# Converting one layer's weights first, by column blocks, and ten chunks of the other layer's a batch later

## The chip, the cores and the metric

The kernel runs on one core of one Trainium2 chip. The metric is the device time of one execution in microseconds (us), the median of several runs. An execution has five engines with queues of their own: PE (matrix multiply; its weight loads are shown apart, as PEld), DVE (vector), ACT (activation functions and copies), POOL (general vector work) and SP, which here only issues DMA transfers. Each engine works its own queue in the order in which the program wrote it; the waits between engines are semaphores.

## The reference, cut to what matters

```python
def _attn_ref(q, k, v):                      # q, k, v: (8, 8, 576, 64) = batch, head, token, width
    scores = np.matmul(q, k.transpose(0, 1, 3, 2)) / np.sqrt(64)
    kth = np.partition(scores, -32, axis=-1)[..., -32:-31]
    scores = np.where(scores >= kth, scores, -1e9)
    attn = np.exp(scores - max); attn /= sum
    return attn @ v

def _moe_ref(x, w_ch1, w_ch2):               # x: (8, 576, 512); w_ch1: 512 x 2048; w_ch2: 2048 x 512
    u = x + np.real(np.fft.fft(np.fft.fft(x, axis=1), axis=2))
    un = (u - mean) / sqrt(var + 1e-6)
    return u + np.maximum(un @ w_ch1, 0.0) @ w_ch2
```

Attention keeps the 32 largest scores of each row; its output, with the heads side by side, goes through the Fourier mix and a two-layer network. The two weight matrices are given as 64-bit floats, while q, k and v have 32 bits.

## The kernel before, in words

**Tiles and steps.** A batch has 8 heads, taken in four pairs; a pair has nine tiles of attention rows (`IN_PAIR`, L292). So a batch has 36 tiles (`PER_BATCH`), all eight have 288 (`N`). The main loop (L1348) takes one step per tile. A step `i` emits, among other things: the score matmuls of tile `i+3` (`scores`, L300) and the copies of them to `S` on ACT; the mask (`mask`, L394: ACT at L397, then POOL at L400) and the exponentials (`expo`, L402, ACT) of an earlier tile; PE's transposes of the result (`transposes`, L411); and on DVE the search for the 32 largest (`top_ops`, L366), which is the last half for tile `i` and the first half for tile `i+1`: four MAX8 (L381) and three MATCH_REPLACE8 (L383) in a step. `bounds` (L386) then makes two small numbers per row on POOL (`nt`), which mask and exponentials need.

In the first batch (`short`, L1353) the exponentials of a step come ahead of the matmuls and the mask follows the search in the same step. From the second batch on, mask and exponentials of tile `i-1` both lie in step `i`, with ACT's part of the mask after the score copies and the exponentials at the end of the step.

**The second half of a batch** follows `T0`, some steps after its last tile: folds, a Fourier transform by matmuls (`dft_tokens`, `dft_channels`), statistics, and then the network. `hidden` (L823) multiplies by `w1` and ACT applies the Relu; `back` (L852) multiplies by `w2`. These network matmuls are units in `queue`, and each step takes as many of them as the planner (`level`, L1321) gives it, so that PE has other work beside the next batch's attention. In the first batch there are no such units yet.

**Weights.** As the matrices have 64-bit numbers, each chunk of 128 rows by 512 columns is loaded raw and converted by six operations (`weight_steps`, L165): `scale_high` and two in `rest` on ACT, `shift` on DVE, and two `join` on POOL. There are 32 chunks, 16 of `w1` and then 16 of `w2`, in the order of rows. Chunk `n` is converted in step `34 * n // 32 + 1` (`start_of`, L1187), so in all but two of the steps 1 to 34 of the first batch. The raw words lie in five slots of one space (`sp1`), and at the end of the step a load for chunk `n + 5` is issued on SP, once the slot is free.

**Centring.** `un` is not centred; instead the mean over the rows is taken off each column of `w1`. `centre(c)` (L1200) does it for 512 columns: 4 matmuls with a matrix of ones, one copy on ACT to `mean`, and 4 subtractions on POOL. Two of the four blocks are centred in the first batch (in steps 19 and 27, a subtraction in each of the four steps after), the others in steps 36 and 37, with all four subtractions of each in step 39 and 40.

**Order.** `at(step, where, fn)` puts work into a plan, and the loop runs it at fixed places of the step: "convert" at the step's head (ACT), "pe" among its matmuls, "shift" after the third operation of the first search half (DVE), "join" inside the mask of the first batch, between ACT's part and POOL's, and "pool" and "load" at the step's end. `parts_of_w2` (L779) makes sums of parts of `w2` for later batches on POOL, from step 50 on.

Of the kernel before, what the change touches and what calls it, by code (L numbers as in the profile page):

```python
# [9 lines left out]
F32 = mybir.dt.float32  # L10
I32 = mybir.dt.int32
# [7 lines left out]
P = 128  # L19
# [45 lines left out]
def kernel(  # L65
# [9 lines left out]
    nc = tc.nc  # L75
    B, H, S, D = q.shape
    DM = H * D
    DF = moe_w_ch1.shape[1]
# [6 lines left out]
    NDT = DM // P  # L85
    NIT = DF // P
# [7 lines left out]
    CW = (2 * P + TAIL, 2 * P)  # L94
# [12 lines left out]
    batp = ctx.enter_context(tc.tile_pool(name="batp", bufs=1))  # L107
# [25 lines left out]
    w1 = const.tile([P, NDT, DF], F32, name="w1", tag="w1")  # L133
    w2 = const.tile([P, NIT, DM], F32, name="w2", tag="w2")
# [21 lines left out]

    def weight_chunks(dst, src, n, wc):
        return [  # L160
            (dst[:, t, c:c + wc], src[P * t:P * (t + 1), c:c + wc])
            for t in range(n) for c in range(0, dst.shape[2], wc)
        ]

    def weight_steps(chunks, space, wc, slots):  # L165

        def words(n):
            o = 2 * wc * (n % slots)
            raw = space[:, o:o + 2 * wc]
            return raw, raw[:, 0:2 * wc:2], raw[:, 1:2 * wc:2]  # L170

        def load(n):
            if n < len(chunks):
                dst, src = chunks[n]
                if moe_w_ch1.dtype == F32:
                    nc.sync.dma_start(out=dst, in_=src)
                else:
                    nc.sync.dma_start(out=words(n)[0].bitcast(I32), in_=src.bitcast(I32))

        def scale_high(n):  # L180
            if moe_w_ch1.dtype == F32:
                return
            nc.scalar.activation(
                out=chunks[n][0], in_=words(n)[2], func=AF.Copy, scale=2.0 ** -112
            )

        def shift(n):
            if moe_w_ch1.dtype == F32:
                return
            bits = chunks[n][0].bitcast(I32)  # L190
            nc.vector.tensor_scalar(
                out=bits, in0=bits, scalar1=3, scalar2=None, op0=ALU.logical_shift_left,
            )

        def rest(n):
            if moe_w_ch1.dtype == F32:
                return
            _, low, high = words(n)
            nc.scalar.activation(
                out=low.bitcast(I32), in_=low.bitcast(U32), func=AF.Copy, scale=2.0 ** -29  # L200
            )
            nc.scalar.activation(out=high, in_=high.bitcast(I32), func=AF.Sign)

        def join(n, part):
            if moe_w_ch1.dtype == F32:
                return
            dst, (_, low, high) = chunks[n][0], words(n)
            bits = dst.bitcast(I32)
            if part == 0:
                nc.gpsimd.tensor_tensor(out=bits, in0=bits, in1=low.bitcast(I32), op=ALU.add)  # L210
            else:
                nc.gpsimd.tensor_tensor(out=dst, in0=dst, in1=high, op=ALU.mult)

        return load, scale_high, shift, rest, join


# [77 lines left out]
    PER_BATCH = NPB * PER_PAIR  # L294
# [249 lines left out]
    folded, y_of, yt_of, us_of, rs_of, unT_of = ({} for _ in range(6))  # L544
# [191 lines left out]
    def channels_first(b, t):  # L736

        rows = ROWS[t]
        ch, col = CHUNK_OF[t]
        if (b, ch) not in unT_of:  # L740
            unT_of[b, ch] = batp.tile(
                [P, NDT, CW[0]], F32, name=f"unT_{b}_{ch}", tag="fold_s" if ch == 0 else "y"
            )
# [427 lines left out]

    sp1 = batp.tile([P, NIT * CW[0]], F32, name="space1", tag="hT")
    WC = 512
    wcs = weight_chunks(w1, moe_w_ch1, NDT, WC) + weight_chunks(w2, moe_w_ch2, NIT, WC)
    n1 = NDT * DF // WC
    AHEAD = 5
    load, scale_high, shift, rest, join = weight_steps(wcs, sp1, WC, AHEAD)
    for n in range(3):
        load(n)
    load_v(0)  # L1180
    load_nat("q", 1)
    for n in range(3, AHEAD):
        load(n)
# [12 lines left out]
    ones = batp.tile([P, P], F32, name="ones", tag="yt")  # L1196
    nc.vector.memset(ones, 1.0 / DM)
    mean_of = {0: batp.tile([P, 2, DM], F32, name="means", tag="fold_d")}

    def centre(c, early):  # L1200
        cols = slice(DM * c, DM * (c + 1))
        cm = ps_s.tile([P, DM], F32, name=f"cm_{c}", tag="sp")
        for dt in range(NDT):
            nc.tensor.matmul(
                cm, lhsT=ones, rhs=w1[:, dt, cols], start=(dt == 0), stop=(dt == NDT - 1)
            )
        if c == DF // DM // 2:

            mean_of[1] = batp.tile([P, 2, DM], F32, name="means_1", tag="x", bufs=2)
        mean = mean_of[2 * c // (DF // DM)][:, c % 2, :]  # L1210
# [12 lines left out]

    for c in range(DF // DM):

        early = c < DF // DM // 2
        at(
            start_of[n1] + 2 + 8 * c if early else PER_BATCH - 2 + c, "pe",
            lambda c=c, early=early: centre(c, early), 3.5,
        )  # L1230

    for kc in range(NK):
        for half in range(2):
            at(
                PER_BATCH + 14 + 2 * kc + half, "pool",
                lambda kc=kc, half=half: parts_of_w2(kc, half),
            )
    for o, place in ((B12, w2_12), (B21, w2_21)):
        at(PER_BATCH + 14, "load2", lambda o=o, place=place: nc.sync.dma_start(
            out=scr[:, o], in_=place  # L1240
        ))

# [63 lines left out]
    queue, waiting, pending, written, now, out_next = [], [], [], set(), [0], []  # L1306
# [41 lines left out]
    while i < N + 4 or plan or queue or sums:  # L1348
# [53 lines left out]
        room = step_us - carry - fixed_cost(i)  # L1402
# [102 lines left out]
```

## Time and profile before

| | us |
|---|---|
| median of 3 runs (1910.49 to 1912.05) | 1911.56 |
| the profiled execution, its own time | 1912.29 |
| the profiled execution, span from first to last instruction | 1910.5 |
| PE busy, of the span | 1797.9 |
| DVE busy | 1584.3 |
| ACT busy | 1209.2 |
| POOL busy | 875.7 |
| the 32 `shift`s on DVE, together | 20.13 |
| one `scale_high` or half of `rest` on ACT, median | 0.66 |
| one `join` on POOL, median | 1.29 |
| one subtraction of `centre` on POOL, median | 1.28 |

The page of a profile has busy times as shares of the whole span. Here that hides that the execution has stretches with different limits, so the answers by stretch ("windows") and the instructions in order of time ("timeline") are read beside it. A time in a row of the timeline is the start in us from the beginning of the span, then the duration, and in square brackets how long the engine was idle ahead of it and which instruction ended that. A line such as `x <- y: 1.4, 1, 1.4` in the waits gives the total, the number and the longest.

In this execution step 1 begins at about 16 us, step 36 at about 219 us, and steps 40 to 49 lie between about 268 and 321 us on ACT.

### The profile page before, as it was taken

To read this page: it belongs to the slowest core of one execution; us is meant where nothing else is said; L and a number is where in the kernel's file an instruction comes from. 1 tells how busy PE (TensorE), PEld (TensorE's weight loads), DVE (VectorE), ACT (ScalarE), POOL (GpSimd) and SP (SyncE) were. 2 spreads that over 40 slices of the span, in tenths; PEclk is the share of its full clock that TensorE was granted. 3 is DMA by queue.
4 is the path that set the end of the run, shared out by engine and by line. 5 is a ranking of instruction groups with operands and counts; after the bars stand their busy time and mean duration, and the time that the engine had idled before them with its cause. 6 is when DMAs were issued, how large, how long until landed. Compare 5 with 4: busy or idle time off the path is not lost.

```text
span 1910.5 us, 28279 instructions
## 1 busy us (share of the span) xinstructions
PE 1797.9 (94%) x9008; PEld 1190.7 (62%) x9008; DVE 1584.3 (83%) x3277; ACT 1209.2 (63%) x3078; POOL 875.7 (46%) x1158
## 2 busy tenths in 40 slices
PE   5567799999999999999999999999999999999999
PEld 3344465474666756766567656667567656767677
DVE  8999989999999999989898898888899888862110
ACT  6878657676766767666676667666676667652100
POOL 4768643555635454345535454355535454341012
PEclk7787899999999999999999999999999999999999
DMA  5333002211104111140014101140013102030132
GB/s 167 103 95 107 20 13 59 90 55 25 47 24 119 31 27 41 42 120 19 19 47 110 46 14 52 42 121 19 19 47 101 51 18 59 23 102 6 50 101 78
DMA packets 184339, 111.34 MB, mean 58 GB/s; under 512 B 125952, under 2 KB 174208, under 8 KB 184192
## 3 DMA queue, kind: packets, MB, share of 16 engines
q1 hardware_dynamic: 183408, 109.33, 20.3%
q8 instruction: 72, 1.18, 0.3%
q14 instruction: 75, 0.61, 0.1%
q10 hardware_dynamic: 784, 0.21, 0.0%
HBM read 93.76 MB, written 15.73 MB: 57 GB/s over the span
## 4 chain that ended last, share of the span: by engine, by line
PE 80%; DVE 8%; ACT 5%; POOL 3%; issue 2%; DMA 1%; SPq 0%; POOLq 0%; DVEq 0%; ACTq 0%
PE hp L832 25%; PE cp L859 10%; PE o L464 8%; PE tpP L427 6%; PE sp L360 6%; PE cw L1029 5%; PE cv L1029 4%; DVE m L381 4%; PE yp L634 3%; PE mp L682 3%; PE cp L898 3%; DVE wk L383 3%; PE sp_t L330 2%; POOL wk L400 1%; ACT wk L406 1%
## 5 line engine op out<-in xcount | busy, mean ns | idle before, releaser
L400 POOL TENSOR_TENSOR wk<-S,wk 128x576 f32<-128x576 f32 x288 | 407.9, 1416 | 772.4 <-ACT wk L397 744.1
L381 DVE MAX8 m<-wk 128x8 f32<-128x576 f32 x864 | 626.3, 749 | 6.1
L832 PE MATMUL hp<-unT,w 128*128 128x256 f32 (+1 forms) x2048 | 538.3, 410 | 2.6 <-ACT unT L750 2.6
L832 PEld LDWEIGHTS hp<-unT,w 128*128 128x128 f32 x2048 | 373.6, 191 | 124.3 <-issue 25.2
L383 DVE MATCH_REPLACE8 wk<-m,wk 128x576 f32<-128x576 f32 x576 | 427.4, 742 | 0.0
L406 ACT ACTIVATE wk<-wk,nt 128x576 f32<-128x576 f32 x288 | 224.9, 781 | 70.8 <-POOL wk L400 66.7
L427 PE MATMUL tpP<-ident,wk 128*128 128x128 f32 x1152 | 182.4, 282 | 69.0 <-ACT wk L406 41.9
L430 ACT COPY PT<-tpP 128x512 f32<-128x512 f32 (+1 forms) x320 | 171.2, 546 | 111.3 <-PE tpP L427 109.0
L859 PE MATMUL cp<-w,hT 128*128 128x512 f32 x512 | 240.6, 598 | 0.0
L397 ACT ACTIVATE wk<-S,nt 128x576 f32<-128x576 f32 x288 | 226.9, 788 | 18.8 <-POOL nt L390 17.6
L427 PEld LDWEIGHTS tpP<-ident,wk 128*128 128x128 f32 x1152 | 140.2, 144 | 141.7 <-ACT wk L406 65.3
L836 ACT ACTIVATE hT<-hp 128x320 f32<-128x320 f32 (+1 forms) x256 | 104.8, 409 | 194.4 <-PE hp L832 192.2
L381 DVE MAX8 m<-S 128x8 f32<-128x576 f32 x288 | 213.7, 742 | 5.2 <-ACT S L334 5.2
L383 DVE MATCH_REPLACE8 wk<-m,S 128x576 f32<-128x576 f32 x288 | 213.5, 741 | 0.0
L464 PE MATMUL o<-PT,v 128*64 128x256 f32 (+3 forms) x1440 | 194.4, 413 | 2.2 <-ACT PT L430 2.2
L363 ACT COPY S<-sp 128x512 f32<-128x512 f32 (+1 forms) x264 | 141.7, 588 | 53.2 <-PE sp L360 53.0
L360 PE MATMUL sp<-kT,qT 64*128 64x512 f32 (+1 forms) x528 | 160.0, 665 | 4.1 <-ACT means L1217 3.3
L464 PEld LDWEIGHTS o<-PT,v 128*64 128x64 f32 x1440 | 111.0, 152 | 73.3 <-issue 15.7
L859 PEld LDWEIGHTS cp<-w,hT 128*128 128x128 f32 x512 | 88.8, 190 | 86.3 <-issue 86.2
L974 POOL TENSOR_TENSOR hT<-hT 128x512 f32<-128x512 f32 x64 | 81.4, 1274 | 101.5 <-ACT hT L836 89.8
L1029 PE MATMUL cw<-w,hT 128*128 128x256 f32 x448 | 106.8, 383 | 2.5 <-POOL nt L390 1.2
L1029 PEld LDWEIGHTS cw<-w,hT 128*128 128x128 f32 x448 | 81.4, 190 | 20.1 <-issue 6.5
(143 smaller groups left out, 2147.2 us busy)
## 6 DMA issues: line engine op xcount, KB each, us to landing
w<-w_parts SPq DMA_DIRECT2D x82, 512.0 KB, 4.4
space<-in_moe_w_ch_dram SPq DMA_DIRECT2D x32, 512.0 KB, 3.5
nat<-in_q_dram SPq DMA_DIRECT2D x128, 64.0 KB, 2.2
v<-in_v_dram SPq DMA_DIRECT2D x128, 64.0 KB, 2.2
out_dram<-x SPq DMA_DIRECT2D x32, 256.0 KB, 2.1
nat<-in_k_dram SPq DMA_DIRECT2D x124, 64.0 KB, 2.1
w_parts<-w_t SPq DMA_DIRECT2D x8, 512.0 KB, 2.9
w_s<-w_parts SPq DMA_DIRECT2D x8, 512.0 KB, 4.9
```

The source lines that it names most:

```text
L360: nc.tensor.matmul(sp[r], lhsT=qT[hd, q_cols], rhs=kT[hd, :], start=True, stop=True)
L381: ops.append(lambda src=src, m8=m8: nc.vector.max(out=m8, in_=src))
L383: ops.append(lambda src=src, m8=m8: nc.vector.match_replace(w, m8, src, NEG))
L397: nc.scalar.activation(out=w, in_=Ssb[i], func=AF.Relu, scale=-FAR, bias=Nt[i][:, 1:2])
L400: nc.gpsimd.tensor_tensor(out=w, in0=Ssb.pop(i), in1=w, op=ALU.subtract)
L406: nc.scalar.activation(out=w, in_=w, func=AF.Exp, bias=Nt.pop(i)[:, 0:1], accum_out=den_t[pair % 3][:, c:c + 1],)
L427: nc.tensor.transpose(tp[:, c, :], p_sb[:, k0 + P * c:k0 + P * (c + 1)], ident)
L430: nc.scalar.copy(out=pt[:, NF * he:NF * (he + 1), col:col + w], in_=tp[:, :, o:o + w])
L464: nc.tensor.matmul(o[D * e:D * (e + 1), c0:c1], lhsT=vv[:, c, e, :], rhs=pt[:, 2 * NF if c == NF else NF * e + c, c0:c1], start=(c == 0), ...
L832: nc.tensor.matmul(hp[:, 0:w], lhsT=w1[:, dt, P * it:P * (it + 1)], rhs=unT[:, dt, 0:w], start=(dt == 0), stop=(dt == NDT - 1),)
L859: nc.tensor.matmul(cp, lhsT=hT[:, it, P * n:P * (n + 1)], rhs=w2[:, it, :], start=(it == 0), stop=(it == NIT - 1),)
L1029: nc.tensor.matmul(dst, lhsT=h()[a][:, kc, :], rhs=rhs_of(kc), start=start and kc == 0, stop=kc == NK - 1, skip_group_check=True,)
```

## The change

The chunks of `w1` are now taken by column blocks (all four row blocks of the first 512 columns, then of the next), so that a block is complete after four chunks. Each block is centred in the first batch: matmuls in steps 7, 12, 18 and 22, and the subtractions two to a step in the steps 9 and 10, 15 and 16, 21 and 22, 23 and 24. No chunk is converted in those steps. The 16 chunks of `w1` and six of `w2` are converted in the first batch (steps 1 to 8, 11 to 14, 17 to 20 and 25 to 30), the last ten chunks of `w2` in steps 40 to 49, one a step. For these ten there are two raw slots in place of five: a part of the buffer that also holds `unT` of the first batch's second chunk, and a buffer under the tag `fold_d`; the load of chunk `n + 2` is issued at the end of the step that converted chunk `n`. The first of the two joins of these ten lies at the end of the step. `parts_of_w2` and two loads with it come one step later.

```diff
-    def weight_chunks(dst, src, n, wc):
+    def weight_chunks(dst, src, n, wc, by_columns=False):
+        every = [(t, c) for t in range(n) for c in range(0, dst.shape[2], wc)]
+        if by_columns:
+            every.sort(key=lambda tc: (tc[1], tc[0]))
+        return [(dst[:, t, c:c + wc], src[P * t:P * (t + 1), c:c + wc]) for t, c in every]
...
+            size = NDT * CW[0]
+            room = batp.tile(
+                [P, 4 * S if ch else size], F32, name=f"unT_{b}_{ch}", tag="y" if ch else "fold_s"
+            )
+            unT_of[b, ch] = room[:, 0:size].rearrange("p (d c) -> p d c", c=CW[0])
+            if b == 0 and ch == 1:
+
+                raws.append(room[:, size:size + 2 * WC])
...
-    start_of = [0] + [34 * n // len(wcs) for n in range(1, len(wcs))]
-    for n, s0 in enumerate(start_of):
-        at(s0 + 1, "convert", lambda n=n: scale_high(n))
-        at(s0 + 1, "convert", lambda n=n: rest(n))
-        at(s0 + 1, "shift", lambda n=n: shift(n))
-        at(s0 + 1, "join", lambda n=n: join(n, 0))
-        at(s0 + 1, "pool", lambda n=n: join(n, 1))
-        at(s0 + 1, "load", lambda n=n: load(n + AHEAD))
+    CONVERT = [
+        *range(1, 9), *range(11, 15), *range(17, 21),
+        *range(25, 25 + NEARLY - n1),
+        *range(PER_BATCH + 4, PER_BATCH + 4 + LATE),
+    ]
+    CENTRE = [(7, 9), (12, 15), (18, 21), (22, 23)]
+
+    raws = []
+
+    def load_late(n):
+        if n >= len(wcs):
+            return
+        if len(raws) < 2:
+            raws.append(batp.tile([P, 2 * WC], F32, name="raw_d", tag="fold_d"))
+        load(n, lambda: raws[(n - NEARLY) % 2])
+
+    for n, s0 in enumerate(CONVERT):
+        at(s0, "convert", lambda n=n: scale_high(n))
+        at(s0, "convert", lambda n=n: rest(n))
+        at(s0, "shift", lambda n=n: shift(n))
+        at(s0, "join" if s0 < PER_BATCH else "pool", lambda n=n: join(n, 0))
+        at(s0, "pool", lambda n=n: join(n, 1))
+        if n < NEARLY:
+            at(s0, "load", lambda n=n: load_early(n + AHEAD))
+        else:
+            at(s0, "load", lambda n=n: load_late(n + 2))
+    for n in range(NEARLY, NEARLY + 2):
+        at(PER_BATCH + 3, "load", lambda n=n: load_late(n))
...
-            s0 = now[0] + 1 + dt if early else now[0] + 3
-            at(s0, "pool", lambda dt=dt: subtract(dt))
+            at(s0 + dt // 2, "pool", lambda dt=dt: subtract(dt))
...
-    for c in range(DF // DM):
-
-        early = c < DF // DM // 2
-        at(
-            start_of[n1] + 2 + 8 * c if early else PER_BATCH - 2 + c, "pe",
-            lambda c=c, early=early: centre(c, early), 3.5,
-        )
+    for c, (s0, s1) in enumerate(CENTRE):
+        at(s0, "pe", lambda c=c, s1=s1: centre(c, s1), 3.5)
```

`NEARLY` is 22 and `LATE` 10.

More of the change, by code (lines that the diff above doesn't have):

```diff
@@ L147, with weight_steps, load @@
     late_now, late_next = [], []
-    def weight_chunks(dst, src, n, wc):
[L160 to L165, printed above, removed]
+    def weight_chunks(dst, src, n, wc, by_columns=False):
[3 more added lines that the diff above has]
+        return [(dst[:, t, c:c + wc], src[P * t:P * (t + 1), c:c + wc]) for t, c in every]
+    def weight_steps(chunks, wc):
+        raw_of = {}
         def words(n):
-            o = 2 * wc * (n % slots)
-            raw = space[:, o:o + 2 * wc]
+            raw = raw_of[n]
             return raw, raw[:, 0:2 * wc:2], raw[:, 1:2 * wc:2]
[L172 to L178, printed above, removed]
+        def load(n, place):
+            dst, src = chunks[n]
+            if moe_w_ch1.dtype == F32:
+                nc.sync.dma_start(out=dst, in_=src)
+            else:
+                raw_of[n] = place()
+                nc.sync.dma_start(out=words(n)[0].bitcast(I32), in_=src.bitcast(I32))
         def scale_high(n):
@@ L740, in channels_first @@
         if (b, ch) not in unT_of:
-            unT_of[b, ch] = batp.tile(
-                [P, NDT, CW[0]], F32, name=f"unT_{b}_{ch}", tag="fold_s" if ch == 0 else "y"
-            )
+            size = NDT * CW[0]
+            room = batp.tile(
+                [P, 4 * S if ch else size], F32, name=f"unT_{b}_{ch}", tag="y" if ch else "fold_s"
+            )
+            unT_of[b, ch] = room[:, 0:size].rearrange("p (d c) -> p d c", c=CW[0])
+            if b == 0 and ch == 1:
+                raws.append(room[:, size:size + 2 * WC])
         shape, name = [P, NDT, P], f"tpu_{b}_{t}"
@@ L1173, with load_early @@
     WC = 512
-    wcs = weight_chunks(w1, moe_w_ch1, NDT, WC) + weight_chunks(w2, moe_w_ch2, NIT, WC)
+    wcs = weight_chunks(w1, moe_w_ch1, NDT, WC, True) + weight_chunks(w2, moe_w_ch2, NIT, WC)
     n1 = NDT * DF // WC
-    AHEAD = 5
-    load, scale_high, shift, rest, join = weight_steps(wcs, sp1, WC, AHEAD)
+    AHEAD, LATE = 5, 10
+    load, scale_high, shift, rest, join = weight_steps(wcs, WC)
+    NEARLY = len(wcs) - LATE
+    def load_early(n):
+        if n < NEARLY:
+            o = 2 * WC * (n % AHEAD)
+            load(n, lambda: sp1[:, o:o + 2 * WC])
     for n in range(3):
-        load(n)
+        load_early(n)
     load_v(0)
@@ L1182 @@
     for n in range(3, AHEAD):
-        load(n)
+        load_early(n)
     nc.sync.dma_start(out=fs, in_=fs_d.ap())
@@ L1186, with centre @@
     nc.sync.dma_start(out=sg, in_=sg_d.ap())
-    start_of = [0] + [34 * n // len(wcs) for n in range(1, len(wcs))]
-    for n, s0 in enumerate(start_of):
-        at(s0 + 1, "convert", lambda n=n: scale_high(n))
-        at(s0 + 1, "convert", lambda n=n: rest(n))
-        at(s0 + 1, "shift", lambda n=n: shift(n))
-        at(s0 + 1, "join", lambda n=n: join(n, 0))
-        at(s0 + 1, "pool", lambda n=n: join(n, 1))
-        at(s0 + 1, "load", lambda n=n: load(n + AHEAD))
+    CONVERT = [
[17 more added lines that the diff above has]
+        at(s0, "pool", lambda n=n: join(n, 1))
+        if n < NEARLY:
+            at(s0, "load", lambda n=n: load_early(n + AHEAD))
+        else:
+            at(s0, "load", lambda n=n: load_late(n + 2))
+    for n in range(NEARLY, NEARLY + 2):
+        at(PER_BATCH + 3, "load", lambda n=n: load_late(n))
     ones = batp.tile([P, P], F32, name="ones", tag="yt")
     nc.vector.memset(ones, 1.0 / DM)
-    mean_of = {0: batp.tile([P, 2, DM], F32, name="means", tag="fold_d")}
-    def centre(c, early):
+    means = batp.tile([P, 2, DM], F32, name="means", tag="fold_d")
+    def centre(c, s0):
         cols = slice(DM * c, DM * (c + 1))
@@ L1206, in centre @@
             )
-        if c == DF // DM // 2:
-            mean_of[1] = batp.tile([P, 2, DM], F32, name="means_1", tag="x", bufs=2)
-        mean = mean_of[2 * c // (DF // DM)][:, c % 2, :]
+        mean = means[:, c % 2, :]
         def subtract(dt):
@@ L1234 @@
             at(
-                PER_BATCH + 14 + 2 * kc + half, "pool",
+                PER_BATCH + 15 + 2 * kc + half, "pool",
                 lambda kc=kc, half=half: parts_of_w2(kc, half),
@@ L1238 @@
     for o, place in ((B12, w2_12), (B21, w2_21)):
-        at(PER_BATCH + 14, "load2", lambda o=o, place=place: nc.sync.dma_start(
+        at(PER_BATCH + 15, "load2", lambda o=o, place=place: nc.sync.dma_start(
             out=scr[:, o], in_=place
```

## The prediction

> **What bounds the kernel now.** First the row of busy tenths on the page, then the windows by stretch, then the waits and the timeline at the places that the change touches.
>
> ```profile
> PE   5567799999999999999999999999999999999999
> DVE  8999989999999999989898898888899888862110
> ...
> 0.00:10.80 10.80, 6.10 (x18) 3.23 (x20) 1.76 (x15) 4.34 (x10) 1.24 (x9) 1.00 0.47 122
> 10.80:230.60 219.80, 140.89 (x713) 85.63 (x710) 215.10 (x437) 175.93 (x410) 156.67 (x156) 0.78 0.34 101
> 230.60:256.60 26.00, 23.03 (x128) 16.94 (x126) 24.58 (x52) 11.04 (x30) 4.70 (x10) 1.00 0.00 1
> ...
> 267.80:320.60 52.80, 50.67 (x249) 32.73 (x248) 51.35 (x106) 39.63 (x107) 20.51 (x24) 1.00 0.08 18
> ...
> 480.00:1880.00 1400.00, 1387.09 (x7004) 934.17 (x7003) 1128.66 (x2343) 860.12 (x2201) 587.82 (x822) 1.00 0.19 53
> ```
>
> A window's row: length; busy us and number for PE, PEld, DVE, ACT, POOL; granted PE clock; DMA share; GB/s. From 10.8 to 230.6 us, the first batch, DVE is busy for 215.1 of 219.8 us while PE has a third of its time free: DVE bounds it. From 480 us on PE is busy for 1387 of 1400 us. Whatever PE loses before that comes off the end one for one. Steps 40 to 49 (267.8 to 320.6) have no free engine but POOL: PE 96%, DVE 97%, ACT 75%.
>
> ```profile
> DVE w L191 <- ACT w L183: 1.4, 1, 1.4
> ...
> 136.55 1.28 POOL L212 TENSOR_TENSOR w<-w,space 128x512 f32<-128x512 f32 x1
> ...
> 137.01 1.11 DVE L191 TENSOR_SCALAR w<-w 128x512 int32<-128x512 int32 x1
> ...
> 228.09 3.70 PE L1204 MATMUL cm<-w,ones 128*128 128x512 f32 x8 [0.84 <-ACT S L352]
> ...
> 235.07 0.76 PE L634 MATMUL yp<-fs,fg 128*128 128x145 f32 x4
> ...
> 281.53 0.78 ACT L406 ACTIVATE wk<-wk,nt 128x576 f32<-128x576 f32 x1
> 282.45 0.65 PE L427 MATMUL tpP<-ident,wk 128*128 128x128 f32 x4 [0.21 <-ACT wk L406]
> 299.19 1.50 ACT L352 COPY S<-sp 64x256 f32<-64x256 f32 x4
> 299.98 0.49 PE L330 MATMUL sp_t<-kt,qT 128*128 128x128 f32 x2 [1.48 <-ACT S L352]
> ```
>
> The first line is DVE's only listed wait between 10.8 and 230.6 us. The pair at 137 us is a shift that ended when POOL's join did: 1.11 us, where most take 0.41. The last four lines are places in steps 41 to 46 where PE already waits for ACT; there ACT has no slack to give.
>
> [...] 32 shifts take 20.13 us, 7.0 more than 32 times 0.41, most of it in eight shifts of 1.1 to 1.4 us. [...] activations in a row overlap[...]. The trace has them 0.56 us apart though each lasts 0.66, so I price a chunk's three at 1.68 us of ACT. [...] The SP rows show loads with gaps of some 5 us between them, a step each.
>
> **First batch: what goes.** DVE begins the search of a new tile every 5.08 us without a shift and every 5.42 with one, 0.34 apart. Ten fewer: 3.4 us. The eight long shifts lie in steps 7, 11, 16, 20, 21, 24, 25 and 29. Steps 16, 21 and 24 have no shift any more, the one in step 20 followed a disturbed step 19, and step 17, behind subtractions, may get one. I take five left at some 0.83 over: 4.2 in place of 7.0, 2.8 us saved (0 to 4). The wait of 1.35 us came from the centring in step 19: its matmuls stood ahead of a tail score on PE, the copy of that (L334) waited 2.92 us, and the next `scale_high` stood behind it on ACT. Steps 7, 12, 18 and 22 have their score matmuls ahead of the centring, as step 27 had, which cost nothing (5.41 us to the next tile). So 1.35 is saved (or, if each of four centrings should hold ACT again, up to 3 lost). Sum: 7.6 us, between 4 and 9.
>
> Subtractions: eight more on POOL in the first batch, two a step (2.56 us) in steps without joins (2.58). They replace each other; POOL is busy for 157 of 220 us. The chunk loads keep their pace, five slots and one a step.
>
> **The seam.** The centring matmuls of steps 36 and 37 (3.60 and 3.70 us on PE) go from there. But DVE runs through to its folds (230.62), and the transform at 235.07 waited 0.76 us for DVE's fold, PE being free. So PE's 7.3 us were under DVE's time and are worth nothing, and the seam simply comes 7.6 us earlier. The subtractions in steps 39 and 40 (4.96 and 4.98 us on POOL) held one set of exponentials for 0.9 us, and PE 0.21: 0.2 us saved.
>
> **Steps 40 to 49: what comes.** Each has one chunk: 1.68 us on ACT at the head of the step, 0.34 on DVE[...], 2.58 on POOL at the end. ACT is busy for 39.6 of 52.8 us; with 16.8 more it is 56.4. Were it packed without a gap, 3.6 us would be lost. It is not packed, since in these steps one chain runs through the whole step: conversion 1.68, score copies 0.95, mask on ACT 0.75 and POOL 1.4, exponentials 0.87, together 5.65 us, against 5.28 for a step now. Queued behind the conversion are the score copies (PE waits for their banks), then the mask, the Relu of `hidden` (PE has three banks), PE's transposes.
>
> I follow the lag through ACT's rows, adding 1.68 a step and taking off the idle time that it covers. At the end of steps 40 to 45 ACT is late by 1.7, 1.1, 2.8, 4.3, 5.4, 4.7 us. Steps 42 and 43 have no idle time to cover it, 45 has. PE is late where it has no slack: 1.2 us at 275.8 (the key copies L284 come late), 2.8 at 282.45, and 6.4 at 299.98, where the copies L352 stand behind the conversion of step 46. After that PE has 3.5 us of slack or more to the exponentials of steps 47 to 49, and ACT's idle time from 320 to 330 us takes its lag back. So 6.5 us of PE are lost, between 3.5 (ACT packed) and 11.
>
> DVE: the shift waits for `scale_high`, so DVE falls back with ACT to some 10 us by step 49. `nt` still comes 4 us or more before ACT wants it, so this costs PE nothing. POOL: its joins come right behind `nt`, and the next mask followed `nt` by 2 to 6 us, so they hold a mask for 0.4 us at worst.
>
> Loads: slot and chunk go round in two steps. From a conversion: copies, masks, `nt`, two joins (2.58), a load (median 3.5 us to landing) come to 11.3 us in two steps, 5.6 a step, about as long as the step itself. On the average I take 0.5 us for this; were landings at the slowest one before, 5.5 us, it would be up to 4.
>
> `w2` in time: the back product that uses chunk 31 is at 337.5 us before; its joins would end by 331, and both move together. Sums of `w2` one step later: the POOL stall of 5.8 us on their store at 333 us moves with them, no gain.
>
> **Sum.** -3.4 - 2.8 - 1.35 - 0.2 + 6.5 + 0.5 = -0.75 us. On the profiled execution's own time, 1912.29 (1.8 around the span of 1910.5, and 0.7 over the median), this gives 1911.5. Two sums of seven, each known to 3 or so, that nearly cancel.
>
> **Rivals.**
> A, the second batch swallows it: PE's queue is dense, ACT has 13.2 us idle in steps 40 to 49, and conversions fill just that. For it: slack of 3 to 5 us at most transposes. Against it: the three places without slack. PE loses 2.5, net about -5: 1907.
> B, the second batch pays more, the case of the other sign: the two raw slots. When a load lands later than some 4 us after its joins, ACT stands at the head of the step, and with it copies, mask and PE, one or two us in four or five steps. Loss 12 in place of 7, net +5: 1917. It decides from a mean landing of 4.2 us on. For it: 5.5 us was seen; against it: little other traffic there (18 GB/s).
> C, the first batch gains nothing: with four centrings of 3.7 us each in DVE's time and conversions close behind, DVE waits 1 us each[...]. Gain 3, net +4: 1916. Against it: step 27.
>
> **How the numbers follow.** Forecast 0.40, with its own range of 1908 to 1916; A 0.30, B 0.25, C 0.05. A measurement of this kernel tells 0.2%, 3.8 us, from no change. Faster: A and a part of 0.05 of the forecast, 0.35. Slower: B, C and 0.05, 0.35. Same: 0.30. The range from 1905 to 1919 takes in A and B with 2 us beyond each.
>
> **What would show it.** Right: the first fold on DVE (230.62) at 222 to 225; DVE's shifts in the first batch at 13 to 14 us; PE busy over steps 40 to 49 falls to about 86%, with waits for ACT's L352, L406 and L284; ACT above 90% there. A: PE waits under 3 us there. B: ACT's `scale_high` waits for DMA. Wrong altogether: the fold no earlier than 228, or waits of PE past 330 us that the kernel before has not.

## The result, and the profile after

The changed kernel takes 1927.43 us (median of 4 runs, 1925.72 to 1928.74), the kernel before 1911.55: a ratio of 1.0083, 95% interval 1.0066 to 1.0101. The forecast was 1911.5 in a range of 1905 to 1919, so the change costs 15.9 us where nothing was expected, and the time lies above the range. The profiled execution has a span of 1926.2 us, against 1910.5 before: 15.7 us are to be found. All functions lie 1 to 34 lines further down in the changed kernel (before's L334, L183 and L352 are L335, L184 and L353).

The row of busy tenths first, from the page of the kernel after:

```profile
PE   5776698989999999999999999999999999999999
DVE  7998988999999999989899988888899988872110
```

A slice is 48.2 us. PE now has an 8 in two slices that held a 9, from 289 to 337 and from 385 to 433 us: two places of loss to look into. Windows over the same stretches of the kernel after (length; then busy us and number for PE, PEld, DVE, ACT, POOL; granted PE clock; DMA share; GB/s):

```profile
10.80:230.60 219.80, 145.93 (x715) 88.18 (x711) 210.10 (x426) 157.52 (x376) 139.15 (x143) 0.77 0.26 76
230.60:256.60 26.00, 24.10 (x113) 17.78 (x110) 22.79 (x46) 9.09 (x25) 4.58 (x4) 0.80 0.00 1
267.80:320.60 52.80, 44.61 (x214) 28.65 (x213) 45.53 (x89) 45.20 (x111) 29.93 (x29) 0.94 0.30 87
480.00:1880.00 1400.00, 1384.97 (x7004) 928.42 (x7003) 1142.36 (x2370) 866.99 (x2222) 597.49 (x834) 1.00 0.19 53
```

In the first batch DVE has 11 fewer instructions, and yet it doesn't finish earlier: 9.7 us of it are idle, where 4.7 were. At the seam the PE clock is 0.80 in place of 1.00. In steps 40 to 49 PE falls from 96% to 84% and ACT rises from 75% to 86%. From 480 us on next to nothing has changed. To see how much each part costs, the same marks are taken in both timelines: DVE's first fold, PE's first `hp` (the first matmul of `hidden`), and ACT's exponentials of tiles 50 and 80.

| stretch | before | after | difference | predicted |
|---|---|---|---|---|
| start to first fold | 230.62 | 231.96 | +1.3 | -7.6 |
| first fold to first `hp` | 25.98 | 28.52 | +2.5 | 0 |
| first `hp` to exponentials of tile 50 | 73.33 | 80.84 | +7.5 | +6.8 |
| exponentials of tile 50 to tile 80 | 161.35 | 165.72 | +4.4 | 0 |
| from there to the end | 1419.22 | 1419.16 | -0.1 | 0 |
| sum | 1910.5 | 1926.2 | +15.7 | -0.8 |

**First batch.** DVE's waits between 10.8 and 232 us, kernel after (us in total, times, longest), where before had one of 1.4:

```profile
DVE m L382 <- ACT S L335: 3.9, 2, 3.5
DVE w L192 <- ACT w L184: 2.7, 3, 2.1
```

Both long ones lie behind the centring in step 22. Rows of the timeline of the kernel after there:

```profile
141.53 6.35 PE L1238 MATMUL cm<-w,ones 128*128 128x512 f32 x8 [2.29 <-ACT S L364]
...
147.72 0.60 PE L428 MATMUL tpP<-ident,wk 128*128 128x128 f32 x4
...
148.36 0.58 ACT L431 COPY PT<-tpP 128x512 f32<-128x512 f32 x1 [6.48 <-PE tpP L428]
...
152.07 0.30 ACT L335 COPY S<-sp_t 128x64 f32<-128x64 f32 x2
152.36 0.76 DVE L382 MAX8 m<-S 128x8 f32<-128x576 f32 x1 [3.53 <-ACT S L335]
...
162.47 1.20 DVE L192 TENSOR_SCALAR w<-w 128x512 int32<-128x512 int32 x1 [2.14 <-ACT w L184]
```

Read it from the top: the product of the centring, `cm`, takes one of the two buffers of the pool of the scores (`ps_s`). PE waits 2.29 us until ACT has copied a score out of one; then the product itself takes 6.35 us, where it took 3.6 to 3.7 before. The transposes stand behind it on PE, ACT has nothing to do for 6.48 us until they come, the copy of the tail score comes after their copies, and DVE waits 3.53 us for that copy. What ten shifts fewer brought (20.13 us of shifts became 15.08) is lost again here.

The product is slow with PE's clock at 0.50 until 146.9 us (0.99 from there to 150), where it was 1.00 in the four products of before; and the clock had fallen before the wait. A window of the kernel after that ends where the wait begins:

```profile
133.30:139.20 5.90, 5.47 (x26) 3.00 (x22) 5.83 (x12) 2.73 (x7) 3.44 (x5) 0.50 0.48 169
```

**Steps 40 to 49.** PE's waits between 256 and 330 us, kernel after:

```profile
PE sp_t L331 <- ACT S L353: 3.1, 1, 3.1
PE hp L838 <- ACT unT L756: 2.1, 1, 2.1
PE tpP L428 <- ACT qT L283: 2.1, 1, 2.1
PE tpP L428 <- ACT kT L285: 1.6, 1, 1.6
PE tpP L428 <- ACT wk L407: 1.4, 2, 0.9
```

Before, the same list has 1.5 for `S`, 2.1 for `unT`, 0.7 for `wk` and none for `qT` and `kT`: 6.0 us are new. The timeline at the longest of them, which is the place that the prediction named (299.98 us before):

```profile
306.22 0.65 ACT L184 ACTIVATE w<-unT 128x512 f32<-128x512 f32 x1
...
307.32 0.66 ACT L203 ACTIVATE unT<-unT 128x512 f32<-128x512 int32 x1
307.88 1.50 ACT L353 COPY S<-sp 64x256 f32<-64x256 f32 x4
...
308.67 0.80 PE L331 MATMUL sp_t<-kt,qT 128*128 128x128 f32 x2 [3.14 <-ACT S L353]
...
309.26 4.47 PE L838 MATMUL hp<-unT,w 128*128 128x320 f32 x8
```

The conversion stands ahead of the score copies, PE waits 3.14 us, and the next eight matmuls take 4.47 us, where eight of this form take 2.3 to 2.4 at every other place of this stretch: the clock is at 0.50 from 307.4 to 314.2 us. The kernel before loses something of this kind too, at another place. Its first 16 matmuls of `hidden`, and then the same 16 of the kernel after, each behind the same wait:

```profile
256.60 6.27 PE L832 MATMUL hp<-unT,w 128*128 128x320 f32 x16 [2.08 <-ACT unT L750]
```

```profile
260.48 4.57 PE L838 MATMUL hp<-unT,w 128*128 128x320 f32 x16 [2.08 <-ACT unT L756]
```

PE's clock over these two was 0.73 and 1.00. So the 7.5 us are 6.0 of new waits and 1.5 of slower matmuls: PE is busy for 72.65 us with the 324 matmul records from the first `hp` to tile 50, and for 71.20 before.

**Tiles 50 to 80.** POOL's long waits while it writes the sums of `w2`, timeline of the kernel after:

```profile
387.15 0.72 POOL L795 TENSOR_TENSOR w_t<-w 128x256 f32<-128x256 f32 x1 [6.48 <-DMA w_parts<-w_t]
...
399.94 0.73 POOL L795 TENSOR_TENSOR w_t<-w 128x256 f32<-128x256 f32 x1 [5.62 <-DMA w_parts<-w_t]
...
411.38 0.73 POOL L795 TENSOR_TENSOR w_t<-w 128x256 f32<-128x256 f32 x1 [4.84 <-DMA w_parts<-w_t]
```

and a PE wait from the timeline of the same kernel behind the first of them:

```profile
390.99 0.66 PE L428 MATMUL tpP<-ident,wk 128*128 128x128 f32 x4 [3.07 <-ACT wk L407]
```

While POOL waits for a store, the mask waits behind it (it starts at 388.63), then the exponentials on ACT (390.07), then PE's transposes.

### The profile page after: what moved, and what is told of

Read it like the earlier page. It is cut to its first block, busy times and chain, and to the rows that moved or that the text cites. A ratio compares the mean times of both kernels' runs of the same rounds, so it can differ in the third digit from the quotient of the medians.

```text
span 1926.2 us, 28278 instructions
## 1 busy us (share of the span) xinstructions
PE 1809.1 (94%) x9008; PEld 1196.7 (62%) x9008; DVE 1588.1 (82%) x3277; ACT 1207.7 (63%) x3078; POOL 875.1 (45%) x1158
## 4 chain that ended last, share of the span: by engine, by line
PE 80%; ACT 7%; DVE 6%; POOL 4%; issue 2%; DMA 1%; SPq 0%; POOLq 0%; DVEq 0%; ACTq 0%
PE hp L838 24%; PE cp L865 11%; PE o L465 8%; PE tpP L428 6%; PE sp L361 6%; PE cw L1035 5%; PE cv L1035 4%; PE yp L635 4%; PE mp L683 3%; PE cp L904 3%; DVE m L382 2%; DVE wk L384 2%; PE sp_t L331 2%; POOL wk L401 2%; ACT wk L407 1%
## 5 line engine op out<-in xcount | busy, mean ns | idle before, releaser
L398 ACT ACTIVATE wk<-S,nt 128x576 f32<-128x576 f32 x288 | 227.0, 788 | 17.0 <-POOL nt L391 15.9
```

Of the source, the lines that this page charges most:

```text
L398: nc.scalar.activation(out=w, in_=Ssb[i], func=AF.Relu, scale=-FAR, bias=Nt[i][:, 1:2])
```

## The experiments

Each is an edit of the kernel after, except where before is named. Times are medians with the range of the runs; ratios are to the kernel before, with 95% intervals. The marks come from one profiled execution each. Three runs have the same code up to the first fold, but for one fill of `w2` at the start of e12 (e7, e9 and e12), and their folds are at 223.84, 226.10 and 224.07, so a single mark is known to about 2 us.

### The first batch: e7 and e1

e7 puts the product into a bank that no score uses.

```diff
-        cm = ps_s.tile([P, DM], F32, name=f"cm_{c}", tag="sp")
+        cm = bank([P, DM], f"cm_{c}")
```

> The changed kernel with the four centring products in the three PSUM banks that nothing else uses much in the first batch, in place of one of the two score banks. Theory A: in step 22 PE stood 2.3 us for a score bank and the next scores for the centring's, and this made DVE wait (6.5 us in the first batch): DVE's waits fall below 3 us, 1923 to 1925. Theory B: it is the half clock and the matmuls' place in PE's order: DVE waits 5 us or more, 1926 to 1928.

1920.52 us (1918.56 to 1921.72), ratio 1.0048 (1.0033 to 1.0062): 6.9 us less than after, and more than the 2.4 to 4.4 us that theory A gave. The list of DVE's waits in the first batch is empty. The product of step 22 in the timeline of e7:

```profile
135.84 3.70 PE L1238 MATMUL cm<-w,ones 128*128 128x512 f32 x8
```

No wait ahead of it, 3.70 us in place of 6.35, and the first fold at 223.84: 8.1 us before that of after, and 6.8 before that of the kernel before, where 7.6 was predicted. The centrings are as many and stand in the same steps, so the sharing of the scores' buffers cost the first batch its gain. What the edit does not separate is the wait for the buffer (2.29 us) from the clock of 0.50 (2.65 us on the product). They came together: in the five kernels that share the buffers in step 22 (after, e2, e3, e6, e8) the product takes 6.35 to 6.55 us, in the four that don't (e7, e9, e10, e12) 3.70.

e1 keeps the order by columns, but centres the last two blocks in steps 36 and 37 as before did (their means lie in a second buffer, as before).

```diff
-    CENTRE = [(7, 9), (12, 15), (18, 21), (22, 23)]
+    CENTRE = [(7, 9), (12, 15), (PER_BATCH, PER_BATCH + 3), (PER_BATCH + 1, PER_BATCH + 4)]
...
-            at(s0 + dt // 2, "pool", lambda dt=dt: subtract(dt))
+            at(s0 + (dt // 2 if c < 2 else 0), "pool", lambda dt=dt: subtract(dt))
```

> The changed kernel, with the centring of the last two column blocks put back to steps 36 and 37 (subtractions in 39 and 40, as before). Theory 1, three separate losses (centring matmuls at half clock hold DVE in the first batch, a cold PE at the seam, ACT in steps 40 to 49): the waits of DVE in the first batch (3.5 and 2.1 us) go and the token transform runs at full clock again, together 8 us: 1919, and the first fold on DVE at about 226. Theory 2, the ten late chunks make the whole loss: no gain, 1926 or more.

1923.0 us (1922.5 to 1925.07), ratio 1.006 (1.0043 to 1.0077). The fold came as expected, at 226.83, and DVE's waits fell to 1.2 us. But the time was 4 us over the expectation: first `hp` to tile 50 took 85.8 us, 5 more than after. Eight subtractions and the joins of the late chunks now meet on POOL there: ACT's exponentials wait 7.7 us for POOL's mask, for 4.2 in after, and PE's transposes 4.8 us for the exponentials, for 1.4.

### The seam: e3 and e4

e3 adds 16 matmuls whose result nothing reads, in steps 36 and 37, where the centring stood.

```diff
+    def again(c):
+        cm = ps_s.tile([P, DM], F32, name=f"cw_{c}", tag="sp")
+        for dt in range(NDT):
+            nc.tensor.matmul(
+                cm, lhsT=ones, rhs=w1[:, dt, DM * c:DM * (c + 1)], start=(dt == 0), stop=(dt == NDT - 1)
+            )
+        return 3.5
+
+    for c in (2, 3):
+        at(PER_BATCH - 2 + c, "pe", lambda c=c: again(c), 3.5)
```

> The changed kernel with 16 matmuls more, whose result nobody reads, where the centring matmuls of steps 36 and 37 had been. Theory 1, they kept PE's clock up: the first transform (30 matmuls for each parity) takes 8.5 us in place of 11 and the time falls by 2.5 to 1925 although PE has 7 us more to do. Rival, the clock there is no cause: the time stays or rises by up to 3, 1927 to 1930.

1928.08 us (1926.2 to 1930.33), ratio 1.0088 (1.0073 to 1.0103): no gain. Windows of the same ten us in after, and then in e3:

```profile
232.00:242.00 10.00, 8.95 (x27) 5.45 (x27) 9.86 (x19) 4.84 (x12) 4.39 (x3) 0.51 0.00 0
```

```profile
232.00:242.00 10.00, 9.21 (x44) 5.52 (x42) 9.66 (x19) 5.32 (x15) 5.06 (x3) 1.00 0.00 0
```

The clock is 1.00 again, and 44 in place of 27 matmul records lie in the ten us. First fold to first `hp` falls from 28.52 to 26.62. The fold itself came 0.9 us later in this execution, which is within what one mark can tell. The regained 1.9 us do not show in the median, and in the trace they are gone by tile 50: that stretch takes 82.6 us in place of 80.8, as the first 16 matmuls of `hidden` are now slow (6.27 us, behind the same wait of 2.08).

e4 is the kernel before without centring of its last two blocks (it leaves that part of the computation out).

```diff
-    for c in range(DF // DM):
+    for c in range(DF // DM // 2):
```

> The kernel before with the centring of the last two column blocks left out (matmuls, copies and subtractions). Theory 1: PE is cold when the first transform begins, which takes some 2.5 us longer: 1914, slower with less work. Rival: less work is free or a gain: 1910.5 to 1911.5.

1913.09 us (1911.09 to 1914.15), ratio 1.0006 (0.9997 to 1.0014): 7.3 us of PE's and 10 us of POOL's work less, and no gain; a loss, as theory 1 has it, is not shown either, as the interval takes in no change. First fold to first `hp` took 27.42 against 25.98. So this work lay under cover, as predicted, and without it the stretch is longer. The place is the first transform: from its first matmul to the first of the second transform it takes 8.4 us in before, 10.1 in e4 and 11.0 in after. (In e3 it is 9.3, at a clock of 1.00 from 232 to 242 us, with a wait of 0.9 for DVE in it.) Over all kernels of this study the stretch takes 25.7 to 26.7 us with matmuls in steps 36 and 37, and 27.0 to 28.5 without (e11 apart, which has more work in it): 0.3 to 2.8 us.

### The ten late chunks: e2, e8 and e10

e2 leaves the loads and conversions of these ten chunks out; the rows of `w2` hold a constant.

```diff
+    nc.gpsimd.memset(w2[:, 6:NIT, :], 0.01)
...
-    for n, s0 in enumerate(CONVERT):
+    for n, s0 in enumerate(CONVERT[:NEARLY]):
...
-    for n in range(NEARLY, NEARLY + 2):
-        at(PER_BATCH + 3, "load", lambda n=n: load_late(n))
```

> The changed kernel with the last ten chunks of w2 left out altogether (no load, no conversion; those rows hold a constant that POOL writes at the start). Theory 1: the 7.5 us of steps 40 to 49 go, and perhaps the 3 us that follow: 1917 to 1920, still well above the kernel before. Theory 2: all 16 us go: 1912 or less.

1916.66 us (1915.56 to 1918.43), ratio 1.0028 (1.0017 to 1.0039), just under the range of theory 1. First `hp` to tile 50 takes 72.9 us, against 80.8 after: the ten cost 7.9 here, for a predicted 7.0. The 4.9 us that are left over the kernel before lie elsewhere: DVE's waits of 6.3 us in the first batch remain, and tile 50 to tile 80 takes 164.8.

e8 keeps the ten loads, a shift on DVE and two operations on POOL for each, but not the three activations on ACT (the rows hold other numbers).

```diff
+        if n < NEARLY:
             at(s0, "convert", lambda n=n: scale_high(n))
             at(s0, "convert", lambda n=n: rest(n))
             at(s0, "shift", lambda n=n: shift(n))
...
+        else:
+            at(s0, "shift", lambda n=n: shift(n, 0))
+            for part in range(2):
+                at(s0, "pool", lambda n=n: product(n))
```

> The changed kernel, where the ten late chunks keep their loads, a shift on DVE and two operations of the same size on POOL, but not the three operations on ACT (so those rows of w2 do not hold the weights, but a constant times other numbers). Theory: ACT at the head of the steps makes the loss of 8 us in steps 40 to 49: 6 to 7 go, 1920 to 1921. Rival, POOL's joins ahead of the mask, DVE's shift or the two raw slots make it: less than 2 go, 1925 or more.

1917.91 us (1916.88 to 1919.55), ratio 1.0038 (1.0024 to 1.0051): 9.5 us less than after, more than the theory's 6 to 7. First `hp` to tile 50 takes 72.9 us, as in e2. Steps 40 to 49 of e8 in the windows:

```profile
267.80:320.60 52.80, 50.88 (x249) 32.59 (x250) 52.25 (x105) 40.18 (x109) 39.52 (x38) 1.00 0.28 87
```

POOL is busier than after (39.5 us), as many bytes move (87 GB/s), and PE has its 96% and a clock of 1.00. So the loads' traffic, POOL's operations and the shifts cost PE nothing here by themselves, and without the 30 activations the loss is gone. In e8 shift and products do not wait for ACT, so what they cost by coming late behind the activations is counted with these. (Nothing reads the raw slots in e8, so the turn of the slots is judged from after itself: none of its ten conversions there waited for a transfer.)

e10 comes with e9's two edits (another bank, and the sums of `w2` a step earlier; see below), and has five chunks late in place of ten; their first two loads are issued five steps later.

```diff
-    AHEAD, LATE = 5, 10
+    AHEAD, LATE = 5, 5
...
-        *range(PER_BATCH + 4, PER_BATCH + 4 + LATE),
+        *range(PER_BATCH + 9, PER_BATCH + 9 + LATE),
```

> As the run with both edits, but five chunks late in place of ten, in steps 45 to 49, five more in steps 31 to 35 of the first batch. Theory, ACT's chain is what the late chunks cost, and the steps 46 to 49 and ACT's idle time behind them can take a part: the first fold comes about 3 us later than with ten (five shifts of 0.34[...]; 226 to 227), first hp to the exponentials of tile 50 falls from 79 to 75 or 76 us: 1915 or so. Rival 1, the cost is per chunk and they all cost the same 0.79: 79 to 75 too, but the fold at 225.5 (only the shifts): 1914. Rival 2, the cost is where the transposes of steps 45 and 46 stand, and five there cost as much as ten: 1920.

1914.96 us (1913.33 to 1916.76), ratio 1.0017 (1.0011 to 1.0024), and 76.5 us from first `hp` to tile 50, where e9 has 80.7 and e12, without any, 72.9: 3.6 us for the five in steps 45 to 49, 4.2 for the five more in 40 to 44. That is the time that theory and rival 1 gave alike, so it doesn't tell them apart; rival 2 is out. Five chunks cost the first batch 0.9 us (fold at 226.97, in e9 226.10), which is below what one mark can tell.

### The sums of `w2`: e5 and e6

e5 is the kernel before with `parts_of_w2` and its loads one step later, and e6 is after with them one step earlier.

```diff
-                PER_BATCH + 14 + 2 * kc + half, "pool",
+                PER_BATCH + 15 + 2 * kc + half, "pool",
...
-        at(PER_BATCH + 14, "load2", lambda o=o, place=place: nc.sync.dma_start(
+        at(PER_BATCH + 15, "load2", lambda o=o, place=place: nc.sync.dma_start(
```

> The kernel before with one part of the change alone: the sums of w2 on POOL and the two loads with them come one step later (51 in place of 50). Theory: this is what costs the changed kernel some 4 us between the exponentials of tile 50 and of tile 80 (161.4 us before, 165.7 after): about 1915. Rival, that stretch is longer because everything ahead of it came late: no change, 1911 to 1912.

> The changed kernel with the sums of w2 and their loads put back by a step, to 50. Theory: 4 us less between tiles 50 and 80: about 1923.5. Rival: no change, 1927.

e5: 1915.62 us (1913.8 to 1916.93), ratio 1.0022 (1.0013 to 1.0032), and tile 50 to tile 80 takes 167.0 us in place of 161.35. e6: 1924.24 (1924.07 to 1925.87), ratio 1.0068 (1.0051 to 1.0084), 3.2 less than after. So one step costs 3 to 4 us in either kernel. Sums and loads were moved together, and are not told apart. POOL's stalls in the timeline of e5, and then of e6:

```profile
375.17 0.73 POOL L789 TENSOR_TENSOR w_t<-w 128x256 f32<-128x256 f32 x1 [6.52 <-DMA w_parts<-w_t]
...
400.84 0.73 POOL L789 TENSOR_TENSOR w_t<-w 128x256 f32<-128x256 f32 x1 [6.43 <-DMA w_parts<-w_t]
```

```profile
350.98 0.74 POOL L795 TENSOR_TENSOR w_t<-w 128x256 f32<-128x256 f32 x1 [5.57 <-DMA w_parts<-w_t]
360.84 0.73 POOL L795 TENSOR_TENSOR w_t<-w 128x256 f32<-128x256 f32 x1 [2.69 <-DMA w_parts<-w_t]
395.02 1.29 POOL L795 TENSOR_TENSOR w_t<-w 128x256 f32<-128x256 f32 x1 [4.08 <-DMA w_parts<-w_t]
```

The one buffer for these sums is stored before it is written anew, so a stall lasts until that store has landed. The stores in question land 2.9 to 3.4 us after their issue, and once 4.6; what makes the long stalls is that they are issued late. In after, POOL has written the buffer at 378.9 us and waits from 380.67 on, but SP has eight loads of `q` to issue first:

```profile
379.49 1.91 SPq L229 DMA_DIRECT2D nat<-in_q_dram  x4
...
383.40 0.38 SPq L797 DMA_DIRECT2D w_parts<-w_t  x1
```

The store lands at 386.73, and POOL goes on at 387.15. In e5 the two stalls above 6 us stand behind eight loads of `q` and eight of `k` in the same way, and in e6 the one of 5.57 behind loads of `v`. The later step has two stalls above 6 us (after: 6.5, 5.6 and 4.8), the earlier has one of 5.6 and shorter ones. PE's waits for the exponentials (total, times, longest) from 330 to 520 us, in e5 and then in e6:

```profile
PE tpP L427 <- ACT wk L406: 9.5, 6, 2.9
```

```profile
PE tpP L428 <- ACT wk L407: 5.1, 5, 2.3
```

In the same window before has 5.3 and after 8.8. Of the 14 kernels, the seven with the earlier step take 161.4 to 163.1 us from tile 50 to tile 80, but for e10 with 164.9, and the seven with the later one 164.8 to 167.0. Within each group the time goes with PE's clock: where the mean of the stretch is 1.00 (before) the earlier step takes 161.4, at 0.99 (e6, e9) 163.0 and 163.1, and at 0.98 (e10) 164.9; the later one takes 165.7 at 0.99 (after) and 167.0 at 0.98 (e5). At the same clock the step makes 2 to 3 us. No run moves the stores alone in SP's queue, so their place there is read from the traces and not tried.

### All together: e9, e12 and e11

e9 has the edits of e7 and e6. e12 has those and e2's too, so it leaves the ten chunks' conversion out.

> The kernel after with the centring product in another bank (worth 6.9 us alone) and the sums of w2 a step earlier (worth 3.2 us alone). Theory, the two places are apart (first batch; 330 to 420 us) and add: 1927.5 - 6.9 - 3.2 = 1917.4 us, first fold at 223.8, exponentials of tile 50 to tile 80 162 to 163 us. Rival, the sums meet the stalls of POOL wherever they fall, and the place of the step was chance: 1920 or more, with tile 50 to tile 80 above 164 us.

> The kernel after with the centring product in another bank, the sums of w2 a step earlier, and without the loads and conversions of the last ten chunks (these rows of w2 are filled with a constant instead). It asks whether the account closes. Theory, three costs that add (6.9, 3.2 and, from the run without the ten chunks, 10.8 us of the median): 1927.4 - 20.9 = 1906.5 us, first fold at 224 to 226, first hp to the exponentials of tile 50 73 us, tile 50 to tile 80 161 to 163 us. Rival, what is gained in the first batch is partly taken back at the seam and by the stalls of POOL, so that the costs overlap: 1910 to 1912, with first fold to first hp 29 us or tile 50 to tile 80 at 165.

e9: 1916.96 us (1915.79 to 1918.97), ratio 1.0028 (1.0017 to 1.0039), for an expected 1917.4: the two add. e12: 1908.98 (1906.13 to 1911.23), ratio 0.9985 (0.9977 to 0.9992), between the theory's 1906.5 and the rival's 1910. Its folds are at 224.07, tile 50 to 80 takes 163.1 us and first fold to first `hp` 27.57. So some 2 us of the three costs overlap (0.7 of the 2.5 is only that the kernel before took 1912.22 in the runs beside e12). Even with the late chunks for nothing, only 3.2 us are won of the 6.6 by which the fold came earlier; 1.6 go at the seam, and 1.8 between tiles 50 and 80, where its clock is 0.99 in place of 1.00.

e11 is a version of the kernel before: its early centrings have their product in another bank, and four unread matmuls fill PE between the transposes of `u` and the first `hp`.

```diff
-        cm = ps_s.tile([P, DM], F32, name=f"cm_{c}", tag="sp")
+        cm = bank([P, DM], f"cm_{c}") if early else ps_s.tile([P, DM], F32, name=f"cm_{c}", tag="sp")
...
+    def warm_up():
+        wu = ps_s.tile([P, DM], F32, name="wu", tag="sp")
+        for dt in range(NDT):
+            nc.tensor.matmul(
+                wu, lhsT=ident, rhs=w1[:, dt, 0:DM], start=(dt == 0), stop=(dt == NDT - 1)
+            )
+        return 0.0
...
+                at(s + 1, "pe", warm_up)
```

> The kernel before with the product of its two early centrings in another bank, and four matmuls whose result nothing reads between the last transposes of u and the first matmuls of hidden, in step 39 (PE work of 1 to 2 us). Theory: DVE's wait of 1.4 us in the first batch goes (first fold at 229.2), and the first hp matmuls run at full clock (2.2 in place of 4.5 us at the place behind the wait for S): 1911.5 - 1.4 - 1.5 = 1908.6. Rival 1, the clock in these stages falls anyway and PE has idle time behind: 1910. Rival 2, the score banks were free when the early centrings took them, as only one of them made DVE wait, and the added matmuls cost their own time: 1912.5.

1910.16 us (1908.47 to 1913.88), ratio 0.9993 (0.9984 to 1.0001). That is the best of the kernels that compute everything, by 1.7 us, but its interval takes in no change. The fold is at 229.27, as expected, yet not for the reason expected: DVE's wait for ACT is still there, at 1.03 us in place of 1.35, and the shifts took 19.14 us in place of 20.13, as they did without this edit in e4 and e5 (19.19 and 19.35). So the other bank is not shown to gain anything here. The unread matmuls did what they were for, though at another place than the expectation says (behind the wait for `S` before has 2.32 us already): the first 16 matmuls of `hidden` take 4.47 us in place of 6.27, and first `hp` to tile 50 71.6 in place of 73.3. The exponentials of tile 50 come 1.75 us earlier than before.

## Why the prediction was wrong

- **Ten fewer shifts: right in kind, somewhat too large.** The shifts of the first batch fell from 20.13 to 15.08 us, in e7 to 14.13, in e9 to 15.69; 13 to 14 was predicted. Of the 2.3 us between the folds of e7 and e9, 1.6 are this difference in shifts. Five long shifts were to be left, and after has eight, of 0.95 to 1.35 us (before: eight of 1.11 to 1.42). In both traces each of the eight began 0.15 to 0.65 us into an operation on POOL and ended 0.28 to 0.30 us after it; so did the one at 137.01 us, which the prediction has end with the join. One that began 0.06 us into a join took 0.41 (124.29 us in after). More of what ties them is not shown.
- **The step that failed: "Steps 7, 12, 18 and 22 have their score matmuls ahead of the centring, as step 27 had, which cost nothing".** It asked where the matmuls stand in PE's queue, and not which buffer they write. In steps 7, 12 and 18 it held: the product took 3.60 us with no wait ahead. In step 18, as in step 27 before, transposes and other matmuls stand for 1.8 us between the score products and the centring; in step 22 it follows them at once. There both buffers held scores that ACT had not copied, and DVE waited 5.7 us behind it, 6.6 in all in the first batch; even the bound ("up to 3 lost") was too low, and the range "between 4 and 9" left that bound out. In place of a gain of 7.6 the fold came 1.3 us later. With another bank the gain came: the fold was 6.8, 4.5 and 6.6 us earlier than before in e7, e9 and e12. Rival C came nearest ("with four centrings of 3.7 us each in DVE's time and conversions close behind, DVE waits 1 us each"), without the buffers; it left a gain of 3 and had a chance of 0.05, where a loss of 1.3 was measured.
- **"PE's 7.3 us were under DVE's time and are worth nothing": the work was, but its absence was not free.** e4 shows that leaving it out gains nothing. The line that it rested on was misread: the 0.76 at 235.07 is the duration of four matmuls and no wait, and PE had score matmuls from 234.02 to 235.14. What was put at nothing is the clock: without these matmuls it stood at 0.51 from 232 to 242 us in after, with unread ones in their place (e3) at 1.00, and the stretch is longer by 0.3 to 2.8 us, 2.5 in the kernel after.
- **Steps 40 to 49: the mechanism was right and the size nearly so.** 6.5 us of PE were predicted from ACT's chain, with places at the key copies, the exponentials and the score copies; 6.0 of new waits and 1.5 of slower matmuls were lost, and e8 shows that it goes with ACT's part. Missing was the clock of 0.50 at the longest wait (2.15 us); and PE's busy share fell to 84%, for some 86%. ACT reached 86% where "above 90%" was expected, as it waits for PE in turn (5.3 us from 267.8 to 320.6). The extra 0.5 us for loads didn't come, nor rival B's late landings: no conversion of the kernel after waited for a load.
- **"Sums of `w2` one step later: the POOL stall of 5.8 us on their store at 333 us moves with them, no gain": wrong.** The step itself is worth 3 to 4 us (e5, e6), and it was put at nothing. POOL's stalls in this stretch grew from 12.9 us in all to 16.9, and fell in other steps of the attention: the moved stores met other loads ahead of them on SP.
- **The sum.** "Two sums of seven, each known to 3 or so, that nearly cancel" made the forecast the difference of one term that stood (+7.5) and one that hung on a bank, and two terms put at nothing came on top (2.5 at the seam, 4.4 between tiles 50 and 80). The -0.75 us were taken off the profiled execution, 0.7 over the median; off the median they give 1910.8. With the bank and the step mended, the change still costs 0.28% (e9): the ten chunks cost some 8 us in steps 40 to 49, and their absence from the first batch brings less.

## What to carry to other kernels

Before adding a product to a matmul queue, look up which buffer its result takes, and who empties the other buffers of that pool: a place behind the urgent matmuls in the queue is no cover when the pool has two buffers and both are in use (in step 22 of after, PE waited 2.29 us for one, and DVE 5.7 us behind it). Work moved from a stretch bound by one engine into one where another has its idle time scattered can cost a good part of its length: ten chunks, 16.8 us of ACT at the prediction's price, cost PE 7.5 to 7.9 us here, in waits and in clock. And a step that only "moves along" is an edit like others where it waits for a transfer: its stalls change with what stands ahead of the transfer in the queue that issues it (POOL's, 12.9 us in before, were 16.9 in after).

## What the runs showed of the hardware

- A wait of PE can cost more than its length: in after, behind 3.14 us of idle time, eight matmuls took 4.47 us in place of 2.32, at a clock of 0.50. The length of the wait doesn't settle it, and what does is not shown. In ten of these kernels the first 16 matmuls of `hidden` take 6.1 to 6.3 us behind a wait of 2.08, in three (after, e6, e9) 4.6 behind the same wait, and in e11, with unread matmuls in place of the wait, 4.47.
- PE work that nothing needs can go with a higher clock: with 16 unread matmuls in steps 36 and 37 (e3) the ten us from 232 on had 1.00, for 0.51 in after. It shortened that stretch by 1.9 us; the next one was longer by 1.8, and the time did not fall.
- The same 22 shifts took 14.13, 15.69 and 14.17 us in three executions (e7, e9, e12): a single execution tells such a sum to no better than 1.6 us.
- The stores that POOL waited for landed 2.9 to 3.4 us after their issue (once 4.6), but stalled it for up to 6.5 us, as eight loads on SP ahead of one took 3.8 us to issue.
